# Two attention blocks on one core: B's head groups spread singly between A's query chunks

## The chip, the cores and the metric

One core of one Trainium2 chip runs the kernel. The metric is the device time of one execution in microseconds; the profile's span runs from the first to the last instruction. The engines are TensorE (PE, matmuls; PEld is its weight load), ScalarE (ACT, exponentials), VectorE (DVE), GpSimd (POOL) and SyncE (SP, which issues the DMAs).

## The reference

Two independent blocks of attention over 2048 tokens, width 1024, 32 heads of 32, all in bf16; the outputs stand side by side.

```python
# A: plain attention
qkv = x @ wqkv                                   # 2048 x 3072
p = softmax(q @ k.T * DH**-0.5); o = p @ v       # every head, 2048 x 2048
a = o @ wo
# B: four segments of 512 tokens, causal inside a segment, with a running memory M, z
for s in range(4):
    a_dot = softmax(qs @ ks.T * scale + causal_mask) @ vs
    a_mem = (phi(qs) @ M) / (phi(qs) @ z + 1e-6)     # phi(t) = t+1 if t>0 else exp(t)
    o[s]  = g * a_mem + (1-g) * a_dot                # g = sigmoid(beta), per head
    M += phi(ks).T @ vs;  z += sum(phi(ks))
b = o @ wo
```

## The kernel before

Heads are handled in groups of four, so that four matmuls of 32 rows or columns share the array: A has eight groups `g`, B eight groups `j` in each of four segments `s`.

Attention of A goes by query chunks of 256. A chunk of a group has 32 tiles of 512 columns (a head, two key tiles). `pack` joins tiles into units of up to three: score matmuls (L680) into three PSUM banks, one exponential on ACT over all of them (L693) into a buffer `P`, and where all four heads of a key group are there, PV and row-sum matmuls (L741, L747) into an accumulator bank. Two slots of three banks (banks 0 to 2 and 3 to 5) alternate, each with three `P` buffers. At the end of a chunk `norm` takes the accumulator: transpose, reciprocal, transpose, multiply on DVE (L766 to L823); only then may the next chunk's PV start in the same bank. A's results go to a DRAM scratch and come back for the output projection. B's groups are alike, with causal masks on POOL (L700): four tiles of 512 columns and eight of 384 per group and segment, in two chunks. In B slot 1 takes two tiles only, since bank 5 is B's second accumulator bank beside bank 7; A has bank 7 alone.

All else is a job that fills PE between scores and PV. A projection (`job_KA`, `job_VA`, `job_KB`, `job_VB`, `job_outB`, `job_outA`) is eight full-array matmuls of 512 columns (16 of 256 for `job_VA`) into bank 6, the only working bank (`X_BANKS`), and one copy on DVE or, in the tail, ACT. K and Q also give squares on POOL and a bound for the exponential's bias (`guard_cols`, `guard_end`), without which a group's exponentials can't start. `job_phi` makes phi of K and Q (an exponential on ACT, two to three DVE steps). `job_mem` reads the memory: matmul (L1096), transpose, reciprocal, transpose, second matmul (L1100), multiply (L1102). `job_M` updates it: four transposes on PE (L1118), a copy, four matmuls (L1129), adds on DVE. Both use bank 6 twice.

The order of attention is `ORDER`: A's groups one by one, with the four segments of B as blocks of eight groups between them, and A's last two groups together chunk by chunk. `plan_jobs` gives each job a release time, a due time and a cost on PE, all on the planned time of attention, and `level` spreads them as evenly as that allows. For B's segment s all eight groups' phi, mem and M, its V and the output of the segment before are released when segment s-1 has ended and due 3 us before segment s starts. `schedule` then lists the instructions of each engine by keys and readiness; scores are urgent, and constants (STICK, PV_ROOM, JOB_AT and so on) weigh staying in one matmul mode, PV and jobs against each other. Each engine executes its list in that order, with semaphore waits.

The lines the change touches:

```python
CAPS = {"A": (3, 3), "B": (3, 2)}
OL_BANKS = {"A": (7,), "B": (7, 5)}
ORDER = [("A", (0,)), ("A", (1,)), ("B", 0), ("A", (2,)), ("B", 1), ("A", (3,)), ("A", (4,)), ("B", 2), ("A", (5,)),
         ("B", 3), ("A", (6, 7))]
```

Of the kernel before, what the change touches and what calls it, by code (L numbers as in the profile page):

```python
# [21 lines left out]
CAPS = {"A": (3, 3), "B": (3, 2)}  # L22
PCAP = (3, 3)
SLOT_BANKS = ((0, 1, 2), (3, 4, 5))
X_BANKS = (6,)
OL_BANKS = {"A": (7,), "B": (7, 5)}
P_RING = (3, 3)

ORDER = [("A", (0,)), ("A", (1,)), ("B", 0), ("A", (2,)), ("B", 1), ("A", (3,)), ("A", (4,)), ("B", 2), ("A", (5,)),
         ("B", 3), ("A", (6, 7))]  # L30
# [86 lines left out]
ROW_LEAD = 0.5  # L117
AHEAD = 4.0
HEAT = 0.43
STICK = 1.5  # L120
OVER = 0.1
PV_ROOM = 4
JOB_AT = 2.5
JOB_SLOPE = 0.4
MARGIN = 1.0
# [227 lines left out]
class _Kernel:  # L353
# [66 lines left out]
    def alloc(self):  # L420
# [30 lines left out]
        self.Pt = [[sb(f"P{s}_{i}", [P, PCAP[s], 512]) for i in range(P_RING[s])] for s in range(2)]  # L451
# [68 lines left out]
    def plan(self):  # L520
        self.plan_constants()
        T = 0.0
        self.seg_start, self.seg_end = {}, {}
        self.sets = {}
        self.att_t = {}
        self.slot_n = 0
        self.ol_now = (None, 0)
        for kind, i in ORDER:
            T0 = T
            if kind == "A":  # L530
                T = self.plan_att_A(i, T)
            else:
                T = self.plan_att_B(i, T)
            for k in (i if kind == "A" else (i,)):
                self.seg_start[(kind, k)], self.seg_end[(kind, k)] = T0, T
        self.T_end = T
        self.plan_prologue()
        self.plan_jobs()
# [50 lines left out]

    def plan_att_A(self, gs, T):  # L590
        tiles = []
        for c in range(S // QC):
            for g in gs:
                groups = list(self.tiles_A())
                for gi, pieces in enumerate(groups):
                    for h in range(4):
                        tiles.append(dict(kind="A", g=g, c=c, h=h, pieces=pieces, set=("A", g, c, gi),
                                          first=gi == 0, last=gi == len(groups) - 1))
        return self.pack(tiles, T)

    def plan_att_B(self, s, T):
        tiles = []
        for j in range(NG):
            for c, groups in reversed(list(enumerate(self.chunks_B()))):
                for gi, pieces in enumerate(groups):
                    for h in range(4):
                        tiles.append(dict(kind="B", g=j, s=s, c=c, h=h, pieces=pieces, set=("B", s, j, c, gi),
                                          first=gi == 0, last=gi == len(groups) - 1))
        return self.pack(tiles, T)

    def pack(self, tiles, T):
        i = 0
        while i < len(tiles):
            slot = self.slot_n % 2
            w = sum(p[2] for p in tiles[i]["pieces"])
            take = [tiles[i]]
            while (len(take) < CAPS[tiles[i]["kind"]][slot] and i + len(take) < len(tiles)):
                t = tiles[i + len(take)]
                if t["g"] != take[0]["g"] or t["kind"] != take[0]["kind"] or t["pieces"] != take[0]["pieces"] and \
                        sum(p[2] for p in t["pieces"]) != w:  # L620
                    break
                take.append(t)
            self.plan_op(take, w, T, slot)
            for t in take:
                self.att_t[(t["kind"], t["g"], t["c"], t.get("s"))] = T
            T += (len(take) * w / 1.2 + 142) / 1000.0
            i += len(take)
        return T
# [149 lines left out]
    def ol_bank(self, t):  # L778
        k = (t["kind"], t["g"], t["c"], t.get("s"))
        if self.ol_now[0] != k:  # L780
            self.ol_now = (k, self.ol_now[1] + 1)
        b = OL_BANKS[t["kind"]]
        return b[self.ol_now[1] % len(b)]
# [424 lines left out]
    def plan_jobs(self):  # L1208
        self.sqB = {}
        st, en = self.seg_start, self.seg_end  # L1210
# [3 lines left out]
        def add(r, d, c, f):  # L1214
            jobs.append((r, d, c, f))
# [6 lines left out]
        for g in range(1, 8):  # L1222
            r = en["A", g - 2] + 2.0 if g > 1 else 1.0
            d = st["A", g] - 7.0
            self.item(r - 10.0, lambda key, g=g: [self.load_WA(g, kq, key) for kq in range(2)])
            for kq in range(2):
                for c in range(4):
                    add(r, d, KQ, lambda key, g=g, kq=kq, c=c: self.job_KA(g, kq, c, key))
            add(r, d, 0.4, lambda key, g=g: self.guard_A(g, key + 2.0))
        for p in range(1, 4):  # L1230
            r = en["A", 2 * p - 3] + 2.0 if p > 1 else 16.0
            d = min(st["A", 2 * p] - 3.0, en["A", 2 * p - 1] - 9.0 if p < 3 else 1e9)
# [4 lines left out]
        for s in range(4):  # L1237
            d = st["B", s] - 3.0
            if s:
                b0, b1 = st["B", s - 1], en["B", s - 1]  # L1240
            else:
                b0, b1 = -1.0, 0.0
            self.item(b0 + (0.1 if s else 4.0), lambda key, s=s: self.load_xB(s, key))
            self.item(b0 + (0.2 if s else 4.1), lambda key, s=s: self.load_WBv(s, 0, key))
            for j in range(8):
                r = b0 + (j + 1) * (b1 - b0) / 8 + 3.0 if s else 14.0
# [3 lines left out]
                if j % 2 == 1:  # L1250
# [23 lines left out]
        t7 = st["A", 7]  # L1274
# [5 lines left out]
        for c in range(8):  # L1280
            r = self.att_t["A", 7, c, None] + 5.0
# [8 lines left out]
        for (r, d, c, f), (t, v) in zip(jobs, self.loads):  # L1290
            self.item(t, f)
# [44 lines left out]
```

## Time and profile before

| | |
|---|---|
| median of 3 runs | 1368.45 us (1364.72 to 1369.27) |
| profiled execution, its own time | 1366.76 us |
| span of it | 1365.0 us |
| PE busy | 1227.0 us (90%) |
| ACT busy | 1194.8 us (88%) |
| DVE busy | 555.2 us (41%) |
| POOL busy | 236.8 us (17%) |
| granted TensorE clock, mean | 0.952 |
| chain that ended last | ACT 45%, PE 40%, DVE 7% |

Busy is the time in which at least one instruction of the engine runs. A granted clock of 1.00 is 2.4 GHz and 0.50 is 1.2 GHz; a value between them is a mix over the stretch. Matmuls overlap, so a busy PE need not be at its peak.

### The profile page before, as it was taken

To read this page: it belongs to the slowest core of one execution; us is meant where nothing else is said; L and a number is where in the kernel's file an instruction comes from. 1 tells how busy PE (TensorE), PEld (TensorE's weight loads), DVE (VectorE), ACT (ScalarE), POOL (GpSimd) and SP (SyncE) were. 2 spreads that over 40 slices of the span, in tenths; PEclk is the share of its full clock that TensorE was granted. 3 is DMA by queue.
4 is the path that set the end of the run, shared out by engine and by line. 5 is a ranking of instruction groups with operands and counts; after the bars stand their busy time and mean duration, and the time that the engine had idled before them with its cause. 6 is when DMAs were issued, how large, how long until landed. Compare 5 with 4: busy or idle time off the path is not lost.

```text
span 1365.0 us, 38206 instructions
## 1 busy us (share of the span) xinstructions
PE 1227.0 (90%) x17312; PEld 527.2 (39%) x17312; DVE 555.2 (41%) x1294; ACT 1194.8 (88%) x924; POOL 236.8 (17%) x403
## 2 busy tenths in 40 slices
PE   5999999899999878999999699989997999888887
PEld 1545433433343323543443234434432343333333
DVE  2233332527432587434332842763246742111211
ACT  1699999998899967799999588889996779999997
POOL 1020220027310025222200011642001630000000
PEclk9999998999899979999999789999996989999999
DMA  9501221201221200002211200121101030000000
GB/s 192 165 22 31 59 66 36 67 19 37 48 56 54 77 5 17 18 23 58 66 44 44 57 13 14 27 48 29 51 21 36 17 111 27 21 25 21 21 22 28
DMA packets 150083, 61.19 MB, mean 45 GB/s; under 512 B 120480, under 2 KB 147104, under 8 KB 149920
## 3 DMA queue, kind: packets, MB, share of 16 engines
q1 hardware_dynamic: 146800, 57.69, 16.2%
q8 instruction: 136, 2.23, 0.7%
q10 hardware_dynamic: 3120, 1.05, 0.3%
q14 instruction: 27, 0.22, 0.1%
HBM read 38.80 MB, written 11.53 MB: 37 GB/s over the span
## 4 chain that ended last, share of the span: by engine, by line
ACT 45%; PE 40%; DVE 7%; SPq 3%; issue 2%; DMA 1%; POOL 1%; DVEq 0%; ACTq 0%; POOLq 0%
ACT P L693 45%; PE ps L885 12%; PE ps L680 9%; PE ps L741 6%; PE ps L747 4%; PE ps L1149 3%; PE ps L1052 3%; PE ps L1038 3%; SPq L955 2%; DVE T L766 1%; DVE T L775 1%; DMA graw<-in_B_beta_dram 1%; DVE PKQ_B L1081 1%; SPq L857 1%; DVE OT_B L1102 1%
## 5 line engine op out<-in xcount | busy, mean ns | idle before, releaser
L693 ACT ACTIVATE P<-ps,bias 128x1536 bf16<-128x1536 f32 (+4 forms) x883 | 1168.9, 1440 | 122.4 <-PE ps L747 98.5
L680 PE MATMUL ps<-KQ_A 32*128 32x256 bf16 x4096 | 278.6, 279 | 31.9 <-ACT P L693 28.8
L747 PE MATMUL ps<-P,onesb 128*32 128x256 bf16 x4864 | 303.5, 276 | 0.0
L741 PE MATMUL ps<-P,V_A 128*32 128x256 bf16 x4096 | 264.7, 282 | 33.0 <-ACT P L693 25.5
L680 PEld LDWEIGHTS ps<-KQ_A 32*128 32x128 bf16 x4096 | 80.4, 93 | 244.8 <-issue 144.3
L741 PEld LDWEIGHTS ps<-P,V_A 128*32 128x32 bf16 x4096 | 109.0, 96 | 159.1 <-issue 85.1
L885 PE MATMUL ps<-xT_B,W_B 128*128 128x512 bf16 x512 | 139.4, 388 | 1.2 <-DVE KQ_B L887 0.7
L893 POOL TENSOR_TENSOR sqA<-KQ_A 128x512 bf16<-128x512 bf16 x56 | 58.1, 1038 | 464.9 <-DVE KQ_A L887 455.3
L700 POOL TENSOR_SCALAR_AFFINE_SELECT P<-P 128x384 bf16<-128x384 bf16 (+2 forms) x254 | 106.8, 439 | 177.6 <-ACT P L693 172.8
L747 PEld LDWEIGHTS ps<-P,onesb 128*32 128x32 bf16 x4864 | 131.2, 98 | 3.3
L885 PE MATMUL ps<-xT_A,W_A 128*128 128x512 bf16 x448 | 123.0, 391 | 3.1 <-DVE cols L910 1.9
L1155 DVE CAST outsb<-ps 128x512 bf16<-128x512 f32 x62 | 42.8, 691 | 189.4 <-PE ps L1149 189.4
L766 DVE STREAM_TRANSPOSE T<-ps 128x256 f32<-128x256 f32 (+1 forms) x152 | 73.4, 486 | 101.9 <-PE ps L747 92.6
L893 POOL TENSOR_TENSOR sqB<-KQ_B 128x512 bf16<-128x512 bf16 x64 | 67.8, 1059 | 222.4 <-DVE KQ_B L887 201.5
L887 DVE CAST KQ_B<-ps 128x512 bf16<-128x512 f32 x64 | 44.1, 690 | 124.0 <-PE ps L885 124.0
L887 DVE CAST KQ_A<-ps 128x512 bf16<-128x512 f32 x56 | 38.7, 691 | 116.1 <-PE ps L885 111.7
L680 PE MATMUL ps<-KQ_B 32*128 32x256 bf16 (+1 forms) x768 | 68.7, 262 | 8.7 <-ACT P L693 7.1
L775 DVE STREAM_TRANSPOSE T<-rc 128x256 f32<-128x256 f32 (+1 forms) x152 | 72.6, 481 | 3.8
L1038 PE MATMUL ps<-Wv_A,xT_A 128*128 128x256 bf16 x512 | 72.6, 283 | 1.6 <-DVE V_A L1042 0.9
L1052 PE MATMUL ps<-Wv_B,xT_B 128*128 128x512 bf16 x256 | 69.1, 390 | 0.3
L1149 PE MATMUL ps<-Wo_B,OT_B 128*128 128x512 bf16 x256 | 69.0, 382 | 0.1
L885 PEld LDWEIGHTS ps<-xT_B,W_B 128*128 128x128 bf16 x512 | 39.8, 98 | 61.0 <-issue 29.2
(81 smaller groups left out, 781.5 us busy)
## 6 DMA issues: line engine op xcount, KB each, us to landing
Wv_B<-in_B_wv_dram SPq DMA_DIRECT2D x8, 1024.0 KB, 5.6
W_B<-in_B_wk_dram SPq DMA_DIRECT2D x32, 256.0 KB, 3.0
W_B<-in_B_wq_dram SPq DMA_DIRECT2D x32, 256.0 KB, 3.0
out_dram<-outsb SPq DMA_DIRECT2D x64, 128.0 KB, 1.8
W_A<-in_A_wqkv_dram SPq DMA_DIRECT2D x14, 256.0 KB, 2.9
ot_a_scratch<-OTst SPq DMA_DIRECT2D x48, 64.0 KB, 1.6
xT_A<-ot_a_scratch SPq DMA_DIRECT2D x6, 512.0 KB, 6.2
Wo_B<-in_B_wo_dram SPq DMA_DIRECT2D x1, 2048.0 KB, 11.9
```

What stands on the lines that cost most here:

```text
L680: ins = e.matmul(out, kap, qap, start=st, stop=True, tile_position=(32 * h, 0), skip_group_check=True)
L693: a = self.act(lambda e: e.activation(dst, src, ACT.Exp, bias=self.bias[:, bc:bc + 1], scale=SCALE), nb * w, key, res + [self.r_bias[bc]], ...
L700: self.pool(lambda e, v=v: e.affine_select(v, v, pattern=[[0, nb], [1, P]], compare_op=ALU.is_ge, fill=0.0, base=0, channel_multiplier=-1) ...
L741: ins = e.matmul(self.ps[32 * h:32 * h + 32, 512 * obk + q0:512 * obk + q0 + nq], vt[:, c0 + 32 * h:c0 + 32 * h + 32], Pt[:, b, off:off + nq],
L747: ins = e.matmul(self.ps[32 * h:32 * h + 32, lcol + q0:lcol + q0 + nq], self.onesb[:, 0:32], Pt[:, b, off:off + nq], start=False, stop=las ...
L766: self.dve(lambda e: e.transpose(T1[:, 0:n], self.ps[:, col:col + n]), n, key, [self.bank[src_bank]], [r1])
L775: self.dve(lambda e: e.transpose(T2[:, 0:n].rearrange("p (b r) -> p b r", r=32), bc), n, key, [rr], [r2])
L885: self.pe(lambda e, i=i: e.matmul(out, wt[:, i, :], xt(i), start=(i == 0), stop=(i == 7)), ncol / 2400.0 + 0.003, key, [rw] + rx(i), [self ...
L893: self.pool(lambda e: e.tensor_tensor(sq[:, :], src, src, ALU.mult), 512, key, [rsrc], [rs], rate=0.5)
L1038: self.pe(lambda e, i=i, t=t, k=k: e.matmul(self.ps[:, 512 * b + 256 * k:512 * b + 256 * k + 256], self.xT[:, i, P * t:P * t + P], self.WA ...
L1052: self.pe(lambda e, i=i: e.matmul(self.ps[:, 512 * b:512 * b + 512], self.xTB[:, i, P * tt:P * tt + P], self.WBv[:, i, :], start=(i == 0), ...
L1149: self.pe(lambda e, j=j: e.matmul(self.ps[:, 512 * b:512 * b + 512], lhs(j), wo(j)[:, 512 * half:512 * half + 512], start=(j == 0), stop=( ...
```

## The change

B's blocks are dissolved. Attention is planned as single units, a chunk of A (`CHUNKS`) or a head group of B, sorted by a position: A's n-th chunk stands at n; B's groups stand 1.4 chunks apart from 10 on, with 2.5 more between segments. A group of B thus runs after one or two chunks of A, from A's 10th chunk to its 61st of 64. Every unit is packed by itself, both slots take three tiles in A and B, and the accumulator is bank 7 for both. The jobs of B get releases and due times by head group: K and Q of a group when the same group of the segment before is done, phi, mem and M around the group's own start, V in two halves. `B_x` and `Wv_B` of a segment load at the second group of the segment before. Costs of phi, mem and M in the plan are larger, and the constants of the list scheduling differ. For A the formulas are those of before, on the new unit times.

```diff
-CAPS = {"A": (3, 3), "B": (3, 2)}
+CAPS = (3, 3)
-OL_BANKS = {"A": (7,), "B": (7, 5)}
+OL_BANKS = (7,)
-ORDER = [...]
+CHUNKS = [(g, c) for g in range(6) for c in range(8)] + [(g, c) for c in range(8) for g in (6, 7)]
+B_FIRST, B_STEP, B_GAP = 10.0, 1.4, 2.5
-ROW_LEAD = 0.5
-AHEAD = 4.0
-HEAT = 0.43
-STICK = 1.5
+ROW_LEAD = 0.4
+AHEAD = 4
+HEAT = 0.5
+STICK = 3
-PV_ROOM = 4
-JOB_AT = 2.5
+PV_ROOM = 5
+JOB_AT = 1.5
...
-        for kind, i in ORDER:
+        units = [(float(n), "A", g, c) for n, (g, c) in enumerate(CHUNKS)]
+        at = B_FIRST
+        for s in range(NSEG):
+            for j in range(NG):
+                units.append((at - 0.5, "B", s, j))
+                at += B_STEP
+            at += B_GAP
+        for _, kind, i, k in sorted(units):
             T0 = T
...
+            T = self.plan_att_A(i, k, T) if kind == "A" else self.plan_att_B(i, k, T)
+            self.st[kind, i, k], self.en[kind, i, k] = T0, T
...
         for g in range(1, 8):
-            r = en["A", g - 2] + 2.0 if g > 1 else 1.0
-            d = st["A", g] - 7.0
+            r = en["A", g - 2, 7] + 2.0 if g > 1 else 1.0
+            d = st["A", g, 0] - 7.0
...
-            self.item(b0 + (0.1 if s else 4.0), lambda key, s=s: self.load_xB(s, key))
-            self.item(b0 + (0.2 if s else 4.1), lambda key, s=s: self.load_WBv(s, 0, key))
+            self.item(rx, lambda key, s=s: self.load_xB(s, key))            # rx = st["B", s - 1, 1] + 1.0
+            self.item(rx + 0.1, lambda key, s=s: self.load_WBv(s, 0, key))
             for j in range(8):
-                r = b0 + (j + 1) * (b1 - b0) / 8 + 3.0 if s else 14.0
+                r = max(en["B", s - 1, j] + 3.0, rx + 12.0) if s else rx + 12.0
+                d = min(SB[j - j % 2] - 5.0, SB[1] - 1.0)                  # SB[j] = st["B", s, j]
...
+            if s:
+                for k in range(8):
+                    add(end + 3.0, SB[0] - 4.0, OUT, lambda key, s=s, k=k: self.job_outB(s - 1, k // 2, k % 2, key))
             for j in range(8):
-                add(r, d, 0.2, lambda key, s=s, j=j: self.job_phi(s, j, key))
+                r = SB[j] - 4.0
+                add(r, SB[j] + 0.0, 0.5, lambda key, s=s, j=j: self.job_phi(s, j, key))
                 if s > 0:
-                    add(r, d, 0.6, lambda key, s=s, j=j: self.job_mem(s, j, key))
+                    add(r, SB[j] + 1.0, 0.9, lambda key, s=s, j=j: self.job_mem(s, j, key))
                 if s < 3:
-                    add(r, d, 0.7, lambda key, s=s, j=j: self.job_M(s, j, key))
+                    add(SB[j], SB[j] + 11.0, 0.9, lambda key, s=s, j=j: self.job_M(s, j, key))
         for k in range(8):
-            add(en["B", 3] + 3.0, self.T_end - 20.0, OUT, lambda key, k=k: self.job_outB(3, k // 2, k % 2, key))
+            add(en["B", 3, 7] + 3.0, self.T_end - 20.0, OUT, lambda key, k=k: self.job_outB(3, k // 2, k % 2, key))
```

## Rows read from the trace of the kernel before

**Rows 1.** Stages: start:end and length, busy us (count) per engine, granted clock, DMA.
```profile
core 0: us, PE busy (x) PEld busy (x) DVE busy (x) ACT busy (x) POOL busy (x), PEclk, DMA share, GB/s
0.00:75.00 75.00, 57.67 (x558) 27.56 (x562) 17.65 (x38) 33.32 (x27) 8.99 (x32) 0.95 0.70 163
75.00:300.00 225.00, 212.47 (x3200) 95.50 (x3192) 75.60 (x185) 221.26 (x159) 28.71 (x27) 0.97 0.18 45
300.00:350.00 50.00, 46.36 (x649) 19.26 (x648) 32.96 (x84) 43.55 (x48) 32.07 (x63) 0.97 0.15 35
350.00:560.00 210.00, 189.25 (x2612) 81.28 (x2608) 114.29 (x275) 177.87 (x146) 47.11 (x89) 0.91 0.16 41
560.00:740.00 180.00, 173.26 (x2482) 76.49 (x2475) 61.03 (x128) 171.65 (x120) 25.55 (x24) 0.99 0.18 45
740.00:1010.00 270.00, 243.87 (x3343) 105.59 (x3340) 129.45 (x307) 228.68 (x180) 53.58 (x90) 0.94 0.13 34
1010.00:1050.00 40.00, 29.29 (x351) 10.57 (x349) 29.84 (x69) 27.64 (x23) 1.04 (x1) 0.70 0.03 8
1050.00:1115.00 65.00, 60.44 (x800) 24.38 (x801) 43.48 (x109) 52.06 (x56) 39.80 (x77) 0.96 0.11 35
1115.00:1365.00 250.00, 214.37 (x3358) 86.59 (x3356) 50.88 (x103) 238.77 (x173) 0.00 (x0) 1.00 0.10 35
sum 1365.00, PE 1226.99 PEld 527.23 DVE 555.19 ACT 1194.79 POOL 236.85; mean PE 136.33 PEld 58.58 DVE 61.69 ACT 132.75 POOL 26.32
```

**Rows 2.** Timeline of PE, line 1096: start us, us, instruction.
```profile
495.53 0.39 PE L1096 MATMUL ps<-PKQ_B,Zb 128*128 128x512 bf16 x1
501.78 0.39 PE L1096 MATMUL ps<-PKQ_B,Zb 128*128 128x512 bf16 x1
```

**Rows 3.** Projection lines of PE, 560 to 740: count, busy us, mean ns, idle before.
```profile
L885 PE MATMUL ps<-xT_B,W_B 128*128 128x512 bf16 x128 | 33.9, 383 | 0.1
L885 PE MATMUL ps<-xT_A,W_A 128*128 128x512 bf16 x64 | 17.1, 382 | 0.0
L1052 PE MATMUL ps<-Wv_B,xT_B 128*128 128x512 bf16 x56 | 15.0, 382 | 0.0
L1149 PE MATMUL ps<-Wo_B,OT_B 128*128 128x512 bf16 x50 | 13.6, 382 | 0.1
L1038 PE MATMUL ps<-Wv_A,xT_A 128*128 128x256 bf16 x80 | 10.6, 274 | 0.0
```

**Rows 4.** The same view, projection lines of PE, 100 to 140.
```profile
L1038 PE MATMUL ps<-Wv_A,xT_A 128*128 128x256 bf16 x115 | 15.9, 274 | 0.0
L885 PE MATMUL ps<-xT_B,W_B 128*128 128x512 bf16 x24 | 6.4, 381 | 0.0
```

**Rows 5.** ACT's groups by shape, whole span: count, busy us, mean ns, idle before.
```profile
L693 ACT ACTIVATE P<-ps,bias 128x1536 bf16<-128x1536 f32 x671 | 981.4, 1583 | 76.1 <-PE ps L747 57.0 <-PE ps L680 11.0 <-DVE bias L937 7.3
...
L693 ACT ACTIVATE P<-ps,bias 128x768 bf16<-128x768 f32 x63 | 56.8, 901 | 8.5 <-PE ps L747 7.4 <-PE ps L680 0.9
...
L1076 ACT ACTIVATE E_B<-KQ_B 128x1024 bf16<-128x1024 bf16 x16 | 17.0, 1060 | 11.6 <-DVE PKQ_B L1081 11.6
```

**Rows 6.** Timeline of ACT, 298 to 320.
```profile
297.08 17.73 ACT L693 ACTIVATE P<-ps,bias 128x1536 bf16<-128x1536 f32 x17
```

**Rows 7.** Timeline of PE, 298 to 303: B's first score matmuls.
```profile
301.79 0.39 PE L680 MATMUL ps<-KQ_B 32*128 32x256 bf16 x6
```

**Rows 8.** Timeline of DVE, 304 to 313.
```profile
305.09 0.69 DVE L887 CAST KQ_A<-ps 128x512 bf16<-128x512 f32 x1 [4.14 <-PE ps L885]
305.93 0.45 DVE L766 STREAM_TRANSPOSE T<-ps 128x256 f32<-128x256 f32 x1
...
307.13 0.42 DVE L805 TENSOR_TENSOR OTst<-ps,T 128x256 bf16<-128x256 f32 x1
...
312.03 0.17 DVE L937 TENSOR_SCALAR bias<-cols 128x1 f32<-128x1 f32 x1
```

**Rows 9.** Timeline of DVE, 563 to 575: first and last of three copies of V_A.
```profile
565.68 0.69 DVE L1042 CAST V_A<-ps 128x512 bf16<-128x512 f32 x1 [1.60 <-PE ps L1038]
...
572.24 0.69 DVE L1042 CAST V_A<-ps 128x512 bf16<-128x512 f32 x1 [2.58 <-PE ps L1038]
```

More of the change, by code (lines that the diff above doesn't have):

```diff
@@ L450, in alloc @@
         self.r_WoA = Res()
-        self.Pt = [[sb(f"P{s}_{i}", [P, PCAP[s], 512]) for i in range(P_RING[s])] for s in range(2)]
+        self.Pt = [[sb(f"P{s}_{i}", [P, CAPS[s], 512]) for i in range(P_RING[s])] for s in range(2)]
         self.r_P = [[Res() for _ in range(P_RING[s])] for s in range(2)]
@@ L522, in plan @@
         T = 0.0
[L523 removed]
+        self.st, self.en = {}, {}
         self.sets = {}
[L525 removed]
         self.slot_n = 0
         self.ol_now = (None, 0)
[L528 to L535 removed]
+        units = [(float(n), "A", g, c) for n, (g, c) in enumerate(CHUNKS)]
[6 more added lines that the diff above has]
+        for _, kind, i, k in sorted(units):
+            T0 = T
+            T = self.plan_att_A(i, k, T) if kind == "A" else self.plan_att_B(i, k, T)
+            self.st[kind, i, k], self.en[kind, i, k] = T0, T
         self.T_end = T
@@ L588, in chunks_B, with plan_att_A, plan_att_B @@
                 [[(0, 0, 256, 0, False), (1, 0, 256, 256, False)], [(2, 0, 256, 0, True), (3, 128, 128, 256, True)]]]
-    def plan_att_A(self, gs, T):
+    def plan_att_A(self, g, c, T):
         tiles = []
[L592 to L598, printed above, removed]
+        groups = list(self.tiles_A())
+        for gi, pieces in enumerate(groups):
+            for h in range(4):
+                tiles.append(dict(kind="A", g=g, c=c, h=h, pieces=pieces, set=("A", g, c, gi),
+                                  first=gi == 0, last=gi == len(groups) - 1))
         return self.pack(tiles, T)
-    def plan_att_B(self, s, T):
+    def plan_att_B(self, s, j, T):
         tiles = []
[L603 to L608, printed above, removed]
+        for c, groups in reversed(list(enumerate(self.chunks_B()))):
+            for gi, pieces in enumerate(groups):
+                for h in range(4):
+                    tiles.append(dict(kind="B", g=j, s=s, c=c, h=h, pieces=pieces, set=("B", s, j, c, gi),
+                                      first=gi == 0, last=gi == len(groups) - 1))
         return self.pack(tiles, T)
@@ L616, in pack @@
             take = [tiles[i]]
-            while (len(take) < CAPS[tiles[i]["kind"]][slot] and i + len(take) < len(tiles)):
+            while len(take) < CAPS[slot] and i + len(take) < len(tiles):
                 t = tiles[i + len(take)]
-                if t["g"] != take[0]["g"] or t["kind"] != take[0]["kind"] or t["pieces"] != take[0]["pieces"] and \
-                        sum(p[2] for p in t["pieces"]) != w:
+                if sum(p[2] for p in t["pieces"]) != w:
                     break
@@ L781, in ol_bank @@
             self.ol_now = (k, self.ol_now[1] + 1)
-        b = OL_BANKS[t["kind"]]
-        return b[self.ol_now[1] % len(b)]
+        return OL_BANKS[self.ol_now[1] % len(OL_BANKS)]
     def norm(self, t, key):
@@ L1235, in plan_jobs @@
                 add(r, d, VJ, lambda key, p=p, tp=tp: self.job_VA(p, tp, key))
-        for s in range(4):
-            d = st["B", s] - 3.0
+        for s in range(NSEG):
+            SB = [st["B", s, j] for j in range(8)]
             if s:
-                b0, b1 = st["B", s - 1], en["B", s - 1]
-            else:
-                b0, b1 = -1.0, 0.0
-            self.item(b0 + (0.1 if s else 4.0), lambda key, s=s: self.load_xB(s, key))
-            self.item(b0 + (0.2 if s else 4.1), lambda key, s=s: self.load_WBv(s, 0, key))
+                end = en["B", s - 1, 7]
+                rx = st["B", s - 1, 1] + 1.0
+            else:
+                end, rx = 10.0, 4.0
+            self.item(rx, lambda key, s=s: self.load_xB(s, key))
+            self.item(rx + 0.1, lambda key, s=s: self.load_WBv(s, 0, key))
             for j in range(8):
-                r = b0 + (j + 1) * (b1 - b0) / 8 + 3.0 if s else 14.0
+                r = max(en["B", s - 1, j] + 3.0, rx + 12.0) if s else rx + 12.0
+                d = min(SB[j - j % 2] - 5.0, SB[1] - 1.0)
                 add(r, d, 0.0, lambda key, s=s, j=j: [self.load_WB(s, j, kq, key - 8.0) for kq in range(2)])
@@ L1290, in plan_jobs @@
         for (r, d, c, f), (t, v) in zip(jobs, self.loads):
+            assert r - 1e-6 <= t and t <= d + 1e-6, (r, t, d, v)
             self.item(t, f)
```

30 lines of the change are left out of this document (12 added, 18 removed).

## The prediction, made before the result was known

> **What bounds the kernel now.** I read the table of stages first, since a whole-span share averages over stages with different limits. ScalarE (ACT), which computes every exponential, is busy 1194.8 of 1365.0 us, so 170.2 us of idle ACT is what any reordering can win [rows 1]. The reader is to see where it lies. Before 75 us it is 41.7 (loads and the first projections), after 1115 us 11.2 (mostly the last output jobs): 52.9 at the ends. The remaining 117.3 us lie between 75 and 1115, and not evenly. From 560 to 740, a stretch of A chunks between B blocks, ACT loses 8.35 of 180 us. Around a B block it loses far more: 12.4 in 40 us just ahead of the last block (1010 to 1050), 12.9 in the 65 us of that block and what follows it, 41.3 in 740 to 1010, 32.1 in 350 to 560.
>
> What happens ahead of a block stands in the timeline of PE. All eight `job_mem`/`job_M` pairs are due at one point. Each goes through the one working bank (bank 6): matmul, a chain of VectorE steps, matmul, transpose, copy, matmul. From the start of one pair to the next it is 6.25 us [rows 2], of which PE works about 1.6. No projection can use that bank meanwhile, PE thins out, and its granted clock is 0.70 over 1010 to 1050, between the levels 1.2 and 2.4 GHz, while it is 0.99 over 560 to 740 [rows 1]. Then the delayed projections crowd the block itself.
>
> Between bursts PE is the second limit: 173.3 of 180 us busy from 560 to 740 [rows 1], while it does 338 matmuls of projections in eights (V_A's 80 are half as wide), so 42.3 jobs, 4.69 per 20 us, with ACT losing 4.6% [rows 3]. From 100 to 140 it does 81.5/8 = 10.2 jobs, 5.1 per 20 us [rows 4], inside the stage 75 to 300 in which ACT loses 3.7 us in all [rows 1].
>
> **The change part by part.** *ACT instructions.* By the loop bounds, A was 692 exponentials (86 in each of six groups, 11 in each of 16 chunks at the end) and becomes 64 x 11 = 704, since a unit now ends its last instruction. B was 191 (mostly six per head group, as slot 1 held two tiles) and becomes 32 x 5 = 160. That is 19 fewer over the same columns. Cost per column and per instruction from two widths: 981.4/671 = 1.463 us for 1536 columns, 56.8/63 = 0.902 for 768 [rows 5], so 0.73 ns a column and 0.34 us an instruction: -19 x 0.34 = -6.5 us. Bounds: 0 and -6.5. New ACT work 1188.3.
>
> *The ends.* Nothing before 75 us changes on the path: 41.7 stay, and the 11.2 at the end too.
>
> *The bursts.* They go: each pair is now planned at its own head group, groups are 1.4 or 2 chunks apart, and a pair's 6.25 us of bank 6 falls among 20 us or more. What is late next is PE. By the order of units, 51 A chunks and 24 B groups run before the fourth segment's first group. With 16384 columns and 11 instructions an A chunk is 15.7 us of ACT, a B group (5120 columns, 5) 5.4; with the 16 phi activations of 1024 (17.0 in all) and eight of half that width (estimated 4) [rows 5] this is 801 + 130 + 21 = 952, less some 27 done before 75 us: 925 us. Jobs due in it: K/Q of A 56, V of A 24, K/Q of B 64, V of B 32, B's output 24, less two done early: 198. The 40 mem and M chains left there take 0.8 us of PE each, 0.4 of a job: 16. That is 214 jobs in 925 us, 4.63 per 20 us. The row nearest in rate and length is 560 to 740: 4.6% of 925 = 42 us. Bounds: 0 (rows 4 did more at no visible loss) and 70 (B groups load PE more).
>
> *B's own price.* In a block ACT loses 12.9 of 65 us [rows 1], but the first block begins without a loss: B's first score is issued at 301.8, and ACT runs from 297.1 on for 17.7 us without a gap, over more than two head groups [rows 6, 7]. A loss builds only when groups follow each other. Singly I cost it 0; bound above: 19.9% of 32 x 5.4 = 34.
>
> *One accumulator bank.* The next chunk's PV matmuls wait until VectorE has read bank 7: from the first transpose at 305.93 to the end of the multiply at 307.55, 1.62 us [rows 8]. Behind that wait on PE only other PV work is held, scores and projections pass by the planner's order. A has that one bank for every chunk, and from 1115 on, where nothing but A is left, ACT loses 11.2 of 250 us, nearly all of it behind the last exponential [rows 1]; cover is the ring of six P buffers, over 7 us of ACT. I take 0. If the cover is gone, it costs 1.62 at each of 64 B chunks, 104 us. The Trainium skill, "Perfetto Trace Analysis", section "Optimizing Tensor Performance", advises rotating independent matmul groups through different banks, so that evacuation lies beside the next group; this edit goes the other way. By that rule the 104 would be paid; A's stretch speaks against it, and it is a rival below.
>
> *A new narrow place.* K and Q of A's group 7 may start when group 5's last chunk is read (they share a slot), and are due before group 7's first chunk. Formerly B's whole last block lay between. Now the order is A5.7, A6.0, A7.0: one chunk. Eight jobs through bank 6 take 3.28 us each where ACT also runs [rows 9]: 26 us; the chunk (15.7) with an estimated 2.5 by which scores run ahead covers 18; then the square, its reduction and the bias follow, from the last copy at 305.09 to the bias at 312.20, 7.1 us, partly behind other work there [rows 8], say 5. Stall 26 - 18 + 5 = 13 us; bounds 5 and 20.
>
> *Queues.* The loads of B_x and Wv_B move to a segment's second group, and `load_WB` moves with its pieces. On SP such a load waits for the last V_B job that reads the buffer; behind it stand A's stores (four buffers, one used per 15.7 us chunk), the W_B loads and B's output stores. Cover is tens of us, cost 0; without it PE lacks weights, which is inside the 70 above.
>
> *The end.* B's last group now lies before the last three chunks, so eight B output jobs and about eight of A's must fit in 47 us; at 5.1 per 20 us 12 fit, the rest partly run in the gap before the final jobs: +5 us (0 to 12).
>
> Planner constants (STICK, PV_ROOM, JOB_AT and others) only change order on PE. Bounds -20 and +20 around the dense loss, value 0: no row shows them.
>
> Sum: 1188.3 + 52.9 + 42 + 13 + 5 = 1301 us of span; 1.8 lies around the span (1366.8 against 1365.0), so 1303. The median of the runs is 1.7 above the profiled time, so I aim at the profiled kind.
>
> **The rivals.** *PE has room (18%).* Dense loss and tail near 0: 1188.3 + 52.9 + 13 + 2 = 1256, 1258 with the rest. For: rows 4. Against: 560 to 740. The Trainium skill, "Perfetto Trace Analysis", section "Identifying the Most-Contended Engine", says that matmul busy time is a poor measure of how near PE is to its limit, and points to the weight loads' share; from 560 to 740 that is 76.5 of 180 us [rows 1], which by the rule leaves room. But ACT did lose 4.6% there, so I keep PE as a limit.
>
> *B's price travels with it (20%).* If single groups lose 19.9% as in a block: + 34, so 1337. For: every block but the first lost from its start. Against: those started in the backlog of a burst.
>
> *Slower: bank 6 as the serial chain (6%).* Every projection and chain uses it. 198 jobs at c us each, 16 pairs at 6.25 and 8 M chains at about half of it, 125, give 198c + 125; the rest of the span (75 + 13 + 230 + 11 + 5) is 334. It decides from c = 4.6 (span 1365); at c = 4.8 the time is 334 + 950 + 125 + 2 = 1411. For: the chains now stand between projections all the time, with VectorE steps that a normalisation can delay. Against: c is 3.28 at 565 to 572 [rows 9].
>
> *Slower: one accumulator bank (4%).* 1303 + 104 = 1407; decides from 1.0 us unhidden per B chunk. For: three normalisations now follow within 20 us. Against: A's last stretch.
>
> **How the numbers follow.** Forecast 50%, PE has room 18%, B's price 20%, the two slower ones 10%, and 2% that all of it cancels. A measurement of this kernel tells 0.3% (4 us) from no change. Faster 0.88, same 0.02, slower 0.10. The range takes in the low rival and the high one with its spread: 1255 to 1348, leaving out the slower cases and a rest.
>
> **What would show it.** Right: 864 exponentials; no stretch with PE's granted clock near 0.7 and ACT near half; ACT idle by stage even, near 4%; one gap of about 13 us ahead of A's group 7, released by the bias. B groups without gaps after them show the one bank harmless. Wrong: gaps on ACT released by PV matmuls at every B group (one bank), projections more than 4.6 us apart throughout (bank 6), or stages at ACT 100% (PE had room).

## The result, and the profile after

The changed kernel takes 1314.72 us (median of 4 runs, 1313.54 to 1321.75) against 1368.78 us for the kernel before on the same chip: 54 us less; the ratio, taken on the means, is 0.9622, 95% interval 0.9583 to 0.9661. The forecast was 1303, range 1255 to 1348.

The page of the changed kernel: span, busy times, and the chain that ended last by engine (an x gives the number of instructions).

```profile
span 1311.8 us, 38085 instructions
...
PE 1196.7 (91%) x17312; PEld 528.3 (40%) x17312; DVE 556.3 (42%) x1294; ACT 1202.3 (92%) x905; POOL 232.0 (18%) x341
...
PE 58%; ACT 32%; DVE 6%; issue 2%; SPq 1%; POOL 1%; DMA 0%; DVEq 0%; ACTq 0%
```

The line of busy times of the kernel before, for its counts:

```profile
PE 1227.0 (90%) x17312; PEld 527.2 (39%) x17312; DVE 555.2 (41%) x1294; ACT 1194.8 (88%) x924; POOL 236.8 (17%) x403
```

PE and DVE have as many instructions as before; ACT has 19 fewer exponentials, and POOL 62 fewer masks. Idle ACT went from 170.2 us [rows 1] to 1311.8 - 1202.3 = 109.5, and the chain moved from ACT (45%) to PE (58%): what ends ACT's waits is mostly matmul work, as it was before, but there is a third as much waiting for PV (below). Where the idle time lies is in the changed kernel's table of stages (start:end, length, busy us and count per engine, granted clock, DMA), cut at its own stages:

```profile
0.00:75.00 75.00, 58.31 (x529) 27.54 (x530) 17.43 (x37) 31.05 (x26) 8.19 (x32) 0.91 0.72 163
75.00:300.00 225.00, 215.65 (x3168) 98.45 (x3166) 84.25 (x196) 216.61 (x160) 46.37 (x53) 1.00 0.21 51
300.00:560.00 260.00, 243.32 (x3717) 110.86 (x3714) 118.32 (x277) 256.02 (x195) 53.34 (x75) 1.00 0.15 39
560.00:700.00 140.00, 128.69 (x1813) 53.89 (x1812) 71.93 (x183) 129.91 (x100) 33.84 (x47) 0.91 0.16 39
700.00:980.00 280.00, 260.44 (x3908) 117.29 (x3910) 138.05 (x322) 273.61 (x206) 55.05 (x75) 0.99 0.15 38
980.00:1020.00 40.00, 31.66 (x348) 12.53 (x344) 11.90 (x24) 21.18 (x16) 8.31 (x8) 0.91 0.37 127
1020.00:1100.00 80.00, 73.95 (x1037) 30.46 (x1031) 33.03 (x78) 73.06 (x55) 9.79 (x16) 0.98 0.05 15
1100.00:1300.00 200.00, 176.01 (x2758) 73.61 (x2753) 77.77 (x174) 198.84 (x152) 17.10 (x36) 0.99 0.07 22
1300.00:1312.00 12.00, 8.68 (x66) 3.64 (x64) 3.60 (x7) 2.01 (x3) 0.00 (x0) 1.00 0.17 56
```

Subtract ACT's busy time (the fourth) from each length. From 75 to 980 ACT idles 8.4, 4.0, 10.1 and 6.4: 28.9 of 905 us, 3.2%. The thinnest place is 980 to 1020, 18.8 of 40 us; 1020 to 1100 loses 6.9 of 80. No stage has the 0.70 of before [rows 1]; the lowest are 0.91, and in cuts of 20 us from 75 us on the lowest is 0.83.

ACT's waits in the changed kernel (awaited work: us in total, times, longest):

```profile
ACT P L688 <- PE ps L742: 32.1, 33, 3.0
ACT P L688 <- DVE bias L931: 25.6, 2, 18.3
...
ACT P L688 <- PE ps L675: 4.0, 7, 1.9
...
ACT E_B L1070 <- DVE PKQ_B L1075: 0.6, 1, 0.6
```

Before, the same kinds were 98.5 (72 times) for PV and row sums (L742, formerly L747), 7.3 for the bias, 14.4 for scores and 12.9 for phi:

```profile
ACT P L693 <- PE ps L747: 98.5, 72, 8.9
...
ACT P L693 <- PE ps L680: 14.4, 27, 1.2
ACT E_B L1076 <- DVE PKQ_B L1081: 12.9, 4, 4.9
ACT P L693 <- DVE bias L937: 7.3, 1, 7.3
```

The exponentials of the changed kernel by shape (count, busy us, mean ns of one, idle before), to be read beside [rows 5]:

```profile
L688 ACT ACTIVATE P<-ps,bias 128x1536 bf16<-128x1536 f32 x672 | 1002.9, 1553 | 72.3 <-PE ps L742 32.0 <-DVE bias L931 25.6 <-PE ps L675 4.0
L688 ACT ACTIVATE P<-ps,bias 128x1152 bf16<-128x1152 f32 x64 | 75.3, 1233 | 0.5
L688 ACT ACTIVATE P<-ps,bias 128x1024 bf16<-128x1024 f32 x64 | 72.1, 1126 | 1.1 <-PE ps L742 0.2
L688 ACT ACTIVATE P<-ps,bias 128x768 bf16<-128x768 f32 x32 | 29.4, 917 | 0.0
L688 ACT ACTIVATE P<-ps,bias 128x512 bf16<-128x512 f32 x32 | 22.7, 709 | 0.0
```

Together 864, as counted. The shapes 1152, 768 and 512 are B's alone, and ACT waits 0.5 us in all ahead of those 128 instructions. B's other 32, the first of each group, are of 1536; in ACT's timeline two of them have a wait ahead, 0.31 and 1.27 us.

The 18.8 stands in the changed kernel's timeline (start us, us, instruction, in brackets idle time before and its releaser). First and last two of the eight K and Q jobs of A's group 7, their last copy, the bias, and the first exponential after it:

```profile
981.06 0.60 PE L879 MATMUL ps<-xT_A,W_A 128*128 128x512 bf16 x2
...
1003.30 1.90 PE L879 MATMUL ps<-xT_A,W_A 128*128 128x512 bf16 x8 [0.79 <-DVE KQ_A L881]
1006.06 1.90 PE L879 MATMUL ps<-xT_A,W_A 128*128 128x512 bf16 x8 [0.85 <-DVE KQ_A L881]
...
1008.22 0.68 DVE L881 CAST KQ_A<-ps 128x512 bf16<-128x512 f32 x1
...
1013.56 0.21 DVE L931 TENSOR_SCALAR bias<-cols 128x1 f32<-128x1 f32 x1
...
1013.81 7.44 ACT L688 ACTIVATE P<-ps,bias 128x1536 bf16<-128x1536 f32 x5 [18.31 <-DVE bias L931]
```

The last jobs go through bank 6 one by one, 2.76 us from start to start, and PE waits for the copy of the one before while ACT has nothing to do.

### The profile page after: what moved, and what is told of

Read it like the earlier page. It is cut to its first block, busy times and chain, and to the rows that moved or that the text cites. A ratio compares the mean times of both kernels' runs of the same rounds, so it can differ in the third digit from the quotient of the medians.

```text
span 1311.8 us, 38085 instructions
## 1 busy us (share of the span) xinstructions
PE 1196.7 (91%) x17312; PEld 528.3 (40%) x17312; DVE 556.3 (42%) x1294; ACT 1202.3 (92%) x905; POOL 232.0 (18%) x341
## 4 chain that ended last, share of the span: by engine, by line
PE 58%; ACT 32%; DVE 6%; issue 2%; SPq 1%; POOL 1%; DMA 0%; DVEq 0%; ACTq 0%
ACT P L688 32%; PE ps L879 15%; PE ps L675 12%; PE ps L736 9%; PE ps L1143 6%; PE ps L742 6%; PE ps L1032 4%; PE ps L1046 4%; SPq L949 1%; DVE T L761 1%; PE ps L919 1%; DVE T L770 1%; DVE cols L904 1%; DVE KQ_A L881 0%; POOL P L695 0%
## 5 line engine op out<-in xcount | busy, mean ns | idle before, releaser
L688 ACT ACTIVATE P<-ps,bias 128x1536 bf16<-128x1536 f32 (+4 forms) x864 | 1177.7, 1443 | 73.9 <-PE ps L742 32.1
L742 PE MATMUL ps<-P,onesb 128*32 128x256 bf16 (+1 forms) x4864 | 294.5, 271 | 0.0
L736 PE MATMUL ps<-P,V_A 128*32 128x256 bf16 x4096 | 255.9, 277 | 22.5 <-ACT P L688 17.1
L695 POOL TENSOR_SCALAR_AFFINE_SELECT P<-P 128x384 bf16<-128x384 bf16 (+1 forms) x192 | 101.4, 541 | 428.4 <-ACT P L688 415.1
L742 PEld LDWEIGHTS ps<-P,onesb 128*32 128x32 bf16 x4864 | 129.9, 97 | 2.4
L675 PE MATMUL ps<-KQ_B 32*128 32x256 bf16 (+1 forms) x768 | 57.5, 255 | 11.9 <-ACT P L688 11.2
## 6 DMA issues: line engine op xcount, KB each, us to landing
Wo_B<-in_B_wo_dram SPq DMA_DIRECT2D x1, 2048.0 KB, 12.1
```

Source lines behind the costliest of these rows:

```text
L675: ins = e.matmul(out, kap, qap, start=st, stop=True, tile_position=(32 * h, 0), skip_group_check=True)
L688: a = self.act(lambda e: e.activation(dst, src, ACT.Exp, bias=self.bias[:, bc:bc + 1], scale=SCALE), nb * w, key, res + [self.r_bias[bc]], ...
L695: self.pool(lambda e, v=v: e.affine_select(v, v, pattern=[[0, nb], [1, P]], compare_op=ALU.is_ge, fill=0.0, base=0, channel_multiplier=-1) ...
L736: ins = e.matmul(self.ps[32 * h:32 * h + 32, 512 * obk + q0:512 * obk + q0 + nq], vt[:, c0 + 32 * h:c0 + 32 * h + 32], Pt[:, b, off:off + nq],
L742: ins = e.matmul(self.ps[32 * h:32 * h + 32, lcol + q0:lcol + q0 + nq], self.onesb[:, 0:32], Pt[:, b, off:off + nq], start=False, stop=las ...
```

## The experiments

Times are medians; each kernel was timed beside the kernel before, and a ratio is to that kernel. Unless said otherwise an edit is made to the changed kernel, whose 1314.7 is then the one to compare with. Four edits move jobs so far that the planner cannot keep every due time; in these it may be up to 3 us late (`d + 3.0`, not shown in the diffs). A line of three dots in a diff stands for lines left out.

**1. The kernel before without the memory chains.** `job_mem` and `job_M` issue nothing and B's results are normalised as in its first segment; the memory term is missing from the output.

```diff
-            if t["s"] == 0:
+            if True:
...
-                    add(r, d, 0.6, lambda key, s=s, j=j: self.job_mem(s, j, key))
+                    add(r, d, 0.6, lambda key: None)
...
-                    add(r, d, 0.7, lambda key, s=s, j=j: self.job_M(s, j, key))
+                    add(r, d, 0.7, lambda key: None)
```

> The kernel before with job_mem and job_M left out (the memory term of B is then missing; phi stays). Theory A, the bursts are what the old order paid for: the 16.8, 17.4 and 12.4 us that ACT idles in front of the three later blocks and part of the crowding behind them go, 45 to 70 us: 1300 to 1323, with PE's granted clock near 1.0 there. Rival, the chains cost only the 0.8 us of PE that each works: 48 x 0.8 = 38 us of PE, of which ACT sees a part, 10 to 25 us: 1343 to 1358.

1296.84 us, ratio 0.9494 (0.9455 to 0.9534): 71.5 us less than the 1368.3 of the kernel before on the same chip. That is just more than was expected, and what its 48 chains cost (24 of each kind) with the addition of their result, although PE works only some 1.6 us in each pair. ACT's waits show the way it reaches ACT: those for PV fall from 98.5 to 43.7 us,

```profile
ACT P L693 <- PE ps L747: 43.7, 40, 4.5
```

and the 12.9 us for phi are gone.

**2. The changed kernel without them.** The same edit, the same term missing.

> The changed kernel with job_mem and job_M left out in the same way. Theory A: spread singly the chains cost little, 5 to 20 us: 1295 to 1310, clearly less than the same edit gains in the kernel before. Rival: the same 10 to 25 us as there.

1292.99 us, 0.9464 (0.9429 to 0.95): 22 us less than with them, just more than expected. Without chains the two kernels are 4 us apart; with them 54. So some 50 of the 54 us are there only because of the chains: in the changed kernel they cost 22 us instead of 71.5. Runs 5 and 7 show that this takes the rest of the change as well.

**3. Chains bunched, attention as changed.** In each segment, phi, mem and M of groups 2 to 7 are planned together at the segment's second group.

```diff
-                r = SB[j] - 4.0
-                add(r, SB[j] + 0.0, 0.5, lambda key, s=s, j=j: self.job_phi(s, j, key))
+                r, dd = (SB[j] - 4.0, SB[j] + 1.0) if j < 2 else (SB[1] + 1.1, SB[1] + 7.0)
+                add(r, dd, 0.2, lambda key, s=s, j=j: self.job_phi(s, j, key))
...                                             # mem and M likewise: (r, dd, 0.2)
```

> The changed kernel with attention interleaved as it is, but phi, mem and M of groups 2 to 7 of each segment planned together right at the segment's second group. Theory A: bursts come back, six pairs instead of eight, in four places (13 us of bank 6 in segment 0, 37 in 1 and 2, 20 in 3); from 12 to 17 us of ACT for eight pairs before, some 9 to 13 each in the middle two and 3 to 6 in the others: 25 to 38 us, 1340 to 1353, with the granted clock falling to 0.7 to 0.8 there. Rival, the gain came from the constants or the packing and not from spreading: within 5 us of 1315.

1364.72 us, 0.9971 (0.9945 to 0.9997): 50 us more than the changed kernel, above what either theory gave. Two 40 us windows of this kernel in which the bunches lie:

```profile
520.00:560.00 40.00, 27.77 (x369) 14.12 (x375) 32.08 (x87) 25.86 (x21) 2.86 (x6) 0.69 0.02 6
...
800.00:840.00 40.00, 25.42 (x316) 10.96 (x312) 31.93 (x88) 25.33 (x21) 3.67 (x7) 0.66 0.14 36
```

and the same windows of the changed kernel:

```profile
520.00:560.00 40.00, 35.23 (x581) 16.00 (x578) 19.74 (x45) 38.93 (x30) 11.13 (x13) 1.00 0.08 19
...
800.00:840.00 40.00, 37.30 (x600) 17.76 (x597) 20.88 (x49) 38.95 (x30) 8.63 (x12) 1.00 0.02 6
```

The burst of before is back in an order of attention that is still interleaved: DVE busy 32 of 40 us, PE thinned out, its granted clock 0.69 and 0.66 (a mix of 1.2 and 2.4 GHz), ACT idle 14.1 and 14.7 us. Three kinds of ACT's waits grow over the whole kernel, by 44.6 us together:

```profile
ACT P L688 <- PE ps L742: 47.5, 44, 4.2
ACT P L688 <- DVE bias L931: 34.3, 3, 23.1
ACT E_B L1070 <- DVE PKQ_B L1075: 21.1, 6, 4.9
```

Nearly half of it, 20.5 us, is ACT's own phi exponentials. By the code phi of a group writes one of two buffers that the chains of the group two before still read. The edit bunches phi too, so its part is not told apart from that of the chains.

**4. Chains at their own groups, attention in blocks.** The eight groups of a segment follow each other again.

```diff
-B_FIRST, B_STEP, B_GAP = 10.0, 1.4, 2.5
+B_FIRST, B_STEP, B_GAP = 16.0, 0.0, 12.0
...
-                    r = max(r, SB[0] - 2.9 + 8.0)
+                    r = max(r, SB[0] - 2.9 + 7.0)
...
-                    add(SB[j], SB[j] + 11.0, 0.9, lambda key, s=s, j=j: self.job_M(s, j, key))
+                    add(SB[j], SB[j] + 4.0, 0.9, lambda key, s=s, j=j: self.job_M(s, j, key))
```

> The changed kernel with B's eight groups of a segment back to back (positions 16, 28, 40, 52), jobs still planned by piece, 864 exponentials as in the changed kernel; the plan's check of due times is loosened by 3 us and M's window shortened from 11 to 4 us so that the order holds. Theory A: a pair every 5.4 us of ACT needs 6.25 us of bank 6, so every block is a burst again: ACT loses 12 to 20 us per block, 45 to 75 in all: 1360 to 1390. Rival, planning by piece is what helps, not the spreading of attention: 1310 to 1330.

1392.26 us, 1.0179 (1.0134 to 1.0224): slower than the kernel before, by a little more than expected. The chains now crowd the block, as its own windows show:

```profile
560.00:600.00 40.00, 27.89 (x338) 12.91 (x345) 34.11 (x93) 23.25 (x23) 10.16 (x21) 0.67 0.20 54
600.00:640.00 40.00, 32.19 (x405) 14.32 (x410) 27.92 (x74) 26.05 (x22) 11.90 (x21) 0.64 0.03 8
```

A chain planned by group is worth nothing here while the groups stand together: of the two halves of the change, neither gains without the other. Both runs keep the constants of the changed kernel; how much of their loss other constants would take back was not tried.

**5 and 6. The constants exchanged.** The changed kernel with the old ones, and the kernel before with the new ones (the same lines the other way round).

```diff
-ROW_LEAD = 0.4
+ROW_LEAD = 0.5
...
-HEAT = 0.5
-STICK = 3
+HEAT = 0.43
+STICK = 1.5
...
-PV_ROOM = 5
-JOB_AT = 1.5
+PV_ROOM = 4
+JOB_AT = 2.5
```

> The changed kernel with the list scheduler's constants of before (ROW_LEAD 0.5, HEAT 0.43, STICK 1.5, PV_ROOM 4, JOB_AT 2.5). ACT is busy 14 us longer in the changed kernel than the prediction worked out. Theory B, the later scores (ROW_LEAD 0.4) let each exponential start a little later behind its forerunner: ACT busy falls from 1202 to 1188 to 1192, time 1300 to 1312 if the modes of PE cost nothing. Rival, the extra ACT time belongs to the mixture of widths: ACT busy stays at 1200 to 1204, time 1310 to 1330.

> The kernel before with the changed kernel's list constants alone. Theory A (spreading is the gain): within 10 us of 1368. Rival (the constants are the gain): 1320 to 1345. Theory B on the ACT work: ACT busy rises from 1195 to some 1208.

Old constants in the changed kernel: 1351.92 us, 0.9874 (0.9852 to 0.9897), 37 us more, outside of both expectations. New ones in the kernel before: 1373.18 us, 1.003 (1.0009 to 1.0052), 4 us more. The constants are no gain of their own, yet in the new order two thirds of it are lost without them. So the gains of the chains (50 us) and of the constants (37) overlap and do not add; the changed kernel with old constants and without chains was not run. One row of the changed kernel with the old ones, 75 to 980:

```profile
75.00:980.00 905.00, 833.09 (x12098) 372.11 (x12097) 375.82 (x934) 837.40 (x632) 168.84 (x238) 0.95 0.16 40
```

ACT idles 67.6 us there against 28.9. ACT's work went the way that theory B said: its busy time fell by 7.8 us in the one kernel (to 1194.5, where 1188 to 1192 was expected) and rose by 13.9 in the other (to 1208.7).

**7. B's second accumulator bank given back**, and with it slot 1 of two tiles in B, since bank 5 belongs to both.

```diff
-CAPS = (3, 3)
+CAPS = {"A": (3, 3), "B": (3, 2)}
...
-OL_BANKS = (7,)
+OL_BANKS = {"A": (7,), "B": (7, 5)}
...                                            # pack and the accumulator look these up by kind, as before
```

> The changed kernel with B's second accumulator bank put back (banks 7 and 5, slot 1 with two tiles in B). Exponentials go back to about six per group: 704 + 160 to 192, up to 28 more at 0.34 us, +5 to +10 us of ACT. Theory, one bank is harmless: 1318 to 1327, no fewer gaps on ACT. Rival, the one bank costs a wait at each B chunk: 1285 to 1308.

1389.94 us, 1.0152 (1.0126 to 1.0178): 75 us more than the changed kernel, and 21 more than the kernel before; neither theory had it. So spread groups and chains with the units and accumulator banks of before gain nothing, at least with these constants. It gave rise to the next.

**8. The two tiles without the second bank.**

```diff
-CAPS = (3, 3)
+CAPS = {"A": (3, 3), "B": (3, 2)}
...                                            # pack looks it up by kind; the accumulator stays in bank 7
```

> The changed kernel with B's slot 1 cut to two tiles, as before the change, but B's accumulator left in bank 7 alone: half of the experiment with two banks, which came out at 1389.9 us with 69.8 us of exponentials waiting for scores. Theory A (the collision in bank 5: A's slot 1 and B's second accumulator want the same bank at each of the 32 single groups): this kernel is rid of it, so only the 27 or so additional exponentials are paid (27 x 0.34 = 9 us) and some thinner cover: 1318 to 1332 us, ACT's waits for scores below 20 us. Rival (two tiles of B in slot 1 are the harm by themselves, since a unit of two tiles is a shorter lead of the scores): above 1365 us, waits for scores above 50 us. Between the two, both have a part, and the time says how much.

1344.78 us, 0.9842 (0.9783 to 0.9901), between the two expectations: some 30 us go with the two tiles, some 45 with the second bank. ACT's waits with two tiles and one bank,

```profile
ACT P L688 <- PE ps L742: 39.3, 37, 2.3
...
ACT P L688 <- PE ps L675: 16.8, 33, 1.3
```

and with the second bank as well:

```profile
ACT P L688 <- PE ps L675: 69.8, 107, 2.8
ACT P L688 <- PE ps L742: 38.9, 41, 3.0
```

The second bank changes nothing about the waits for PV (38.9 and 39.3) and adds 53 us of waits for scores. An explanation would be that A's scores for slot 1 must wait until B's accumulator in bank 5 is read. It is not shown: by the order of the exponentials in the two traces, an estimate since the trace does not name the slot, 31 of the 69.8 us lie ahead of slot 1 and 39 ahead of slot 0. But 176 of the 878 exponentials run out of the planned order with the second bank, and none with one bank. ACT runs its list in order, so with the second bank the list scheduler itself let units of one slot pass units of the other. How this adds up to 45 us is open. Of the 30 us for two tiles, 7.6 are longer ACT work (1209.9 against 1202.3), 12.8 more waits for scores and 7.2 more waits for PV.

**9. The narrow place covered by B.** Groups 5 to 7 of the third segment are moved between A's group 5 and group 6.

```diff
-                units.append((at - 0.5, "B", s, j))
+                units.append((at - 0.5 if (s, j) < (2, 5) or s == 3 else 47.3 + 0.01 * j, "B", s, j))
```

> The changed kernel with three groups of B (groups 5 to 7 of the third segment) moved to between A's group 5 and group 6, so that 16 us of ACT more lie between the release of K and Q of group 7 and their use; the plan's check of due times is loosened by 3 us. Theory: the gap of 18.3 us that the bias ends shrinks to under 4, of which 10 to 16 us reach the end: 1299 to 1306. Rival, the backlog of PE jobs only moves and ACT waits elsewhere: 1311 to 1318.

1334.27 us, 0.9746 (0.9727 to 0.9765): 20 us more, where fewer were expected. The timeline of ACT in this kernel:

```profile
979.96 2.33 ACT L688 ACTIVATE P<-ps,bias 128x768 bf16<-128x768 f32 x2 [2.27 <-PE ps L742]
983.45 2.91 ACT L688 ACTIVATE P<-ps,bias 128x512 bf16<-128x512 f32 x3 [1.16 <-PE ps L742]
987.09 2.33 ACT L688 ACTIVATE P<-ps,bias 128x768 bf16<-128x768 f32 x2 [0.73 <-PE ps L742]
...
1020.09 12.24 ACT L688 ACTIVATE P<-ps,bias 128x1536 bf16<-128x1536 f32 x8 [12.07 <-DVE bias L931]
```

The gap shrinks from 18.3 to 12.1, but of the three groups of B that now stand in a row only the first runs without a wait: ACT waits for PV in the second (2.27 us) and the third (1.16 and 0.73), and in the chunk of A behind it (three times about 1 us, not shown). Waits for PV rise from 32.1 to 45.2 us in all. ACT's work is 3.8 us longer (1206.1).

**10. The narrow place begun earlier.** Q of group 7 goes first, and three of its four jobs no longer wait for group 5's last chunk but for chunks already read; its weights load earlier to match.

```diff
-                holds([r for x in self.r_KQA[g % 2] for r in x], "KQ", g)
+                holds(self.r_KQA[g % 2][0] + [self.r_KQA[g % 2][1][t["c"] // 2] for t in take], "KQ", g)
...
-            for kq in range(2):
+            for kq in (1, 0) if g == 7 else (0, 1):
...
-                    add(r, d, KQ, lambda key, g=g, kq=kq, c=c: self.job_KA(g, kq, c, key))
+                    r1 = en["A", 5, 5] + 2.0 if (g, kq) == (7, 1) and c < 3 else r
+                    add(r1, d, KQ, lambda key, g=g, kq=kq, c=c: self.job_KA(g, kq, c, key))
```

> The changed kernel with three of the eight K/Q projections of A's group 7 released earlier: Q of chunks 0 to 5 goes into columns that group 5 has read by then, so Q is made first, three of its four jobs from group 5's sixth chunk on; five jobs instead of eight stay in the narrow place (the plan's check of due times is loosened by 3 us). Theory: the 18.3 us gap shrinks by 3 x 2.8 = 8 us to about 10, span 1303 to 1309, the rest as it was. Rival, as when three B groups were moved there: PE has no free time in that stretch, the gap shrinks and as much is lost elsewhere: 1312 to 1325.

1310.44 us, 0.9578 (0.9542 to 0.9614): between the two expectations and 4 us below the changed kernel, but the intervals overlap, so that it is better is not shown. The gap is 13.1 us instead of 18.3; 8 us were expected to go, and 5 went:

```profile
1011.52 5.94 ACT L688 ACTIVATE P<-ps,bias 128x1536 bf16<-128x1536 f32 x4 [13.10 <-DVE bias L931]
```

**11. A neighbouring order.**

```diff
-B_FIRST, B_STEP, B_GAP = 10.0, 1.4, 2.5
+B_FIRST, B_STEP, B_GAP = 10.0, 1.45, 2.1
```

> The changed kernel with B's groups 1.45 chunks apart and 2.1 more between segments (instead of 1.4 and 2.5), a neighbour of the same order in which a few groups stand one chunk later; the plan's check of due times loosened by 3 us. If the gain is that of spreading, the time is within 10 us: 1305 to 1325. If the changed kernel is a lucky point among orders of the same kind, it is far worse: 1330 to 1355.

1329.72 us, 0.9714 (0.9679 to 0.9748): 15 us more, just over the one expectation and at the lower edge of the other. The changed kernel is the better of the two, and some 15 of its 54 us hang on the exact spacing; one neighbour was tried.

**12. ROW_LEAD alone back to 0.5.**

> The changed kernel with ROW_LEAD 0.5 alone. If the lead of the scores is what made each exponential longer, ACT busy falls from 1202 by 5 to 10 us; if the other constants (STICK, PV_ROOM) did, it stays within 2. The time: theory B 1305 to 1313; rival, all PE constants act together and the order of PE work decides: 1315 to 1335.

1321.26 us, 0.9677 (0.962 to 0.9735): a median 6.5 us higher, but the intervals overlap, so that it is slower is not shown. ACT's work falls by 13 us to 1189.4, and the time does not fall with it: idle ACT rises from 109.5 to 129.6, waits for PV from 32.1 to 54.9. So this constant is what made ACT's work longer, and taking it back doesn't pay. The exponentials of 1536 columns in this run:

```profile
L688 ACT ACTIVATE P<-ps,bias 128x1536 bf16<-128x1536 f32 x672 | 990.8, 1561 | 87.7 <-PE ps L742 52.6 <-DVE bias L931 29.2 <-PE ps L675 5.1
```

A single one is no shorter than in the changed kernel (1561 against 1553 ns), yet together they are busy 12 us less. What differs is how they follow each other: in the changed kernel 130 of the 864 exponentials start 50 to 150 ns behind the end of the one before, where others overlap with it; with ROW_LEAD 0.5 it is 11. By the code it says how long before the end of the running exponential the next scores are due. The other four (HEAT, STICK, PV_ROOM, JOB_AT) hold the remaining 30 of the 37 us together; which of them was not tried.

## Why the prediction was right, and where its terms were off

The mechanism was right: most of the loss came from the bursts of chains, and spreading them together with the groups removes most of it (runs 1 to 4). That the time came out so near was partly luck: errors of the terms cancel, and the constants, which the prediction put at nothing, had to fit the order. In the span: ACT work 1202.3 instead of 1188.3 (+14.0); ends and the end 55.1 instead of 57.9 (-2.8); the dense stretch 28.9 instead of 42 (-13.1); the gap ahead of group 7 18.3 instead of 13 (+5.3); and 7.5 that no term held, in the rest of 980 to 1100 (+7.5). That is +10.9 on 1301.

- *ACT instructions.* The count was exact, and the direction was wrong: 7.5 us more instead of 6.5 less. [rows 5] give 1583 ns for one exponential of 1536 and 1463 of busy time for each, an overlap of 120 ns on average; after, it is 1553 and 1002.9/672 = 1492, an average of 61. So each exponential became no longer; fewer of them overlap with the one before (run 12). Where two exponentials do overlap, it is by 111 ns before and 110 after, in the median of each trace. The Trainium skill, "ScalarE: Activation LUTs", section "What ACT_TABLE_LOAD costs", puts the overlap of back-to-back activations at about 93 ns; these traces show somewhat more. ROW_LEAD alone moves ACT's busy time by 12.9 us in the changed kernel; all constants together move it by 7.8 there and by 13.9 in the kernel before (runs 5 and 6).
- *The bursts.* Right, by runs 1 to 4. That the one working bank is what makes chains wait is seen in PE's waits of the kernel before, where L1102 is a chain's last read of that bank, and L1096 and L1118 are the first work of the next chain in it (us in total, times, longest):

```profile
PE ps L1118 <- DVE OT_B L1102: 12.2, 13, 1.8
PE ps L1096 <- DVE OT_B L1102: 6.1, 5, 2.2
```

  Ahead of the fourth block no projection has a matmul between these two:

```profile
1010.75 0.82 PE L1149 MATMUL ps<-Wo_B,OT_B 128*128 128x512 bf16 x3
1042.69 0.61 PE L885 MATMUL ps<-xT_A,W_A 128*128 128x512 bf16 x1
```

  No run gave the chains a second bank, so the bank's part in the 71.5 us is not measured by itself. The prediction set the 6.25 us of a pair beside the clock of 0.70 in 1010 to 1050; but the fourth segment has no `job_M`, and its eight `job_mem` start 3.3 to 4.3 us apart there. The pairs, 5.5 to 8.6 us apart, stand ahead of the second and third block. The step that put each pair at its own group as the remedy was incomplete: run 4 does that and is slower than before. It is the pair with room beside it that is cheap, and the chains still cost 22 us in all, not nothing (run 2).
- *The dense stretch.* 42 lay between what the two sets of constants give, 28.9 and 67.6, both inside the bounds 0 to 70. The loss is not even, as the signs of being right had it: from 1.5% in 300 to 560 to 7.2% in 560 to 700.
- *Planner constants.* The most mis-sized term: 0, with bounds of 20 either way, where they are worth 37 us here and nothing in the kernel before. With the old ones the time is 1352 (run 5), outside the range, so that the forecast held is luck in this term. Run 6 bears out that the kernel before gave no sign of it: there the same constants change the time by 4 us.
- *B's own price* is near 0 for single groups: 0.5 us of waits ahead of 128 of its 160 exponentials and 1.6 ahead of the other 32. What a group costs in the chunk of A behind it is not told apart from the rest of the dense stretch. Run 9 shows the other half of the argument: where three groups follow each other, the first has no wait and the next two have.
- *One accumulator bank.* Not only harmless: the second one costs some 45 us in this order (runs 7 and 8). The Trainium skill, "Perfetto Trace Analysis", section "Optimizing Tensor Performance", advises rotating matmul groups through banks; here the second bank also serves the scores of slot 1, and the waits for PV were the same with it and without (38.9 and 39.3).
- *The narrow place.* Eight jobs took 27.8 us (981.1 to 1008.9; 26 predicted), ACT's cover was 14.4 (981.1 to 995.5; 18), the bias followed after 4.9 (5): 18.3. The cover was the mis-sized part: less of the chunk A6.0 was left to ACT when the first job started.
- *The rivals.* PE has room: 700 to 980 comes near it (ACT idle 2.3%), the whole doesn't. B's price travels: refuted, the whole dense stretch loses less than the 34 us that it added. Bank 6 as the serial chain: the eight copies ahead of group 7, where bank 6 does decide, take (1008.2 - 983.9)/7 = 3.5 us each, below the 4.6 needed throughout. One accumulator bank: refuted, ACT waits 32.1 us for PV in all.

## What to carry to other kernels

A short job whose steps wait on each other through one buffer can cost more than the work in it when many are due at once, and a third of that when each has other work beside it: 71.5 us fell to 22 here with the same chains. Spread the jobs and what they belong to together, for either alone gave nothing here (runs 3 and 4). When the order changes, try the scheduler's constants with it (37 us here), and expect that a neighbouring plan can be some 15 us off, as the one tried here was. A second buffer that another consumer also uses can cost more than it saves: some 45 us here.

## What the runs showed that was not expected

- ACT's busy time is no fixed amount of work: for the same 905 instructions it was between 1189.4 and 1206.7 us by the order and constants alone, since it depends on how many neighbours overlap, and the kernel with 1189.4 was no faster than the one with 1202.3.
- With a burst of chains PE's granted clock is 0.66 or 0.69 over 40 us (run 3). But 560 to 700 of the changed kernel has 0.91 without such a burst and with PE busy 128.7 of 140 us. Cut finer, the low clock lies around single groups of B, which start at 568 and 654 there, and PE has fewer matmuls in these cuts than in the 141 and 174 of the 10 us ahead of each, at 1.00:

```profile
570.00:580.00 10.00, 8.29 (x89) 2.56 (x86) 6.64 (x17) 9.79 (x9) 2.91 (x6) 0.66 0.03 9
660.00:670.00 10.00, 8.74 (x93) 3.29 (x93) 6.39 (x21) 8.54 (x7) 1.00 (x2) 0.66 0.01 2
```

  Why the clock falls at these groups and hardly at those from 700 to 980 is open.
